# A broadcast maximum by way of DRAM instead of a matrix product, in a linear-attention and gated-FFN kernel

## The chip, the cores and the metric

The kernel runs on one core of one Trainium2 chip. The metric is the device time of one execution in microseconds, median of several runs. The kernel before takes 1002.14 us (three runs, 1001.49 to 1002.65).

The engines, by their names in the profile: PE is TensorE (matrix products; PEld is its weight load), DVE is VectorE, ACT is ScalarE, POOL is GpSimd, and SP is the sync engine, which here issues every DMA, in the order in which they are written. PSUM is the memory that PE writes products to, in eight banks; SBUF is the memory of the other operands.

## The reference

Linear attention with two softmaxes, then a gated feed-forward block, all in fp32:

```python
# q, k, v: (8 batches, 8 heads, 576 rows, 64)
q_s = exp(q - max(q, -1));  q_s /= sum(q_s, -1) + 1e-9
k_s = exp(k - max(k, 2));   k_s /= sum(k_s, 2) + 1e-9      # over the 576 rows, for each column
attn = einsum('bhsd,bhde->bhse', q_s, einsum('bhsd,bhse->bhde', k_s, v))
x = attn.transpose(0, 2, 1, 3).reshape(4608, 512)
xn = x / sqrt(mean(x*x, -1) + 1e-6) * rms_g
g = xn @ w_gate                                            # 512 x 1536
out = (g * sigmoid(g) * (xn @ w_val)) @ w_out              # 1536 x 512
```

The weights lie in DRAM as 64-bit words, which the kernel converts by itself.

## The kernel before

The 4608 rows are worked in nine blocks j of 512 rows, and the 1536 hidden columns in twelve slices of 128. A step s = 12 j + slice of the feed-forward part consists of f1.s.0 and f1.s.1 (gate and value, L839), twelve products each, and f2.s (the second product, L878). To get fp32 precision from the faster format (fp32r), every operand is split in a high part and a remainder: w_hi and w_lo for a slice of gate and value weights, o_hi and o_lo for the output weights, h_hi and h_lo for the hidden values, q_hi and q_lo for the queries, x_hi and x_lo for the block's input. A product is then three passes (high x high, high x low, low x high). The high parts are copies (L328), by default on ACT; the remainders are differences of two SBUF tensors (L816, L824, L860), by default or by the order on POOL. f2 is split when h_hi and h_lo of its step are in the order; for steps 0 to 3 they are not, and f2 multiplies the fp32 operands natively.

Between f1 and f2 stand g_mul (L844: gate from PSUM times the row factor, on DVE), silu (L848, ACT) and h_mul (L851: value from PSUM times that, DVE). f1 has two PSUM banks (ps_gv), one for gate and one for value, so that f1.s+1.0 waits for g_mul.s and f1.s+1.1 for h_mul.s.

Attention goes by batch b and pair of heads g (four pairs, 28 pairs in batches 1 to 7). For each, k_load fetches k into 116 partitions of five rows each, k_max (L461) takes the maximum of each partition's rows, k_tr (L486) transposes the 128 columns of the two heads to partitions, and k_top (L491) gives kx, one maximum for each of 128 columns, one to a partition. Every partition then needs all 128 of them in a row. Before, k_diag (L495, recorded as L333, on ACT) multiplies an identity matrix by kx, and k_rows (L500) multiplies a matrix of ones by that diagonal on PE, in native fp32; the result is read from PSUM by k_sub (L506, DVE), which subtracts it from k. k_exp (L510) takes the exponential, k_mm (L518) multiplies by v with a column of ones for the sum, and k_eps, k_rec and kv_hi, kv_lo (in batches 0 and 1: kv_norm0) normalise the result. q goes a similar way: q_max, q_half, q_max2, q_sub, q_exp, q_sum, q_half2, q_sum2, q_rec, q_mul, q_t, and q_x multiplies it with the normalised k-v product. x_sq, x_acc, n_sum and the steps n_t to n_cols give the row factors; store scales the block and writes it out.

In batches 2 to 7 the products of k are bundled in k_seg(m), one bank of PSUM each: k_mm of pair m - 2, k_rows of pair m - 1, k_tr of pair m. In batch 1 they are separate steps.

The order of the whole work is written out by hand, as a list of step names in a string (ORDER, some 2,800 names). Each engine executes its own steps in the order of the list; steps on different engines wait for each other's data and buffers alone. A suffix names the engine: `:A` ACT, `:D` DVE, `:P` POOL. conv_mul, conv_shift, conv_sign, conv_low and conv_add convert the weights during block 0; load_w loads them; warm is a product without use that fills PE's time.

Of the kernel before, what the change touches and what calls it, by code (L numbers as in the profile page):

```python
# [22 lines left out]
constants exp_table k_load.0.0 q_load0.0.0 v_ones.0.0 warm.9 k_load.0.2 kv_zero0.0 v_load.0.0 v_ones.0.2 v_ones.0.3  # L23
v_ones.0.1 kv_zero0.1 k_load.0.3 kv_zero.4 q_load0.0.3 kv_zero.5 kv_zero.6 kv_zero.7 k_load.0.1 kv_zero.0 q_load0.0.1
kv_zero.1 kv_zero.2 k_max0.0.0 v_load.0.2 kv_zero.3 q_max0.0.0 q_load0.0.2 k_tr.0.0 warm.2.0 k_top.0.0 q_sub0.0.0:P
v_load.0.3 k_diag.0.0:A k_rows.0.0 k_sub.0.0 warm.2.1 g_load q_exp.0.0 v_load.0.1 q_sum0.0.0 k_exp.0.0 load_w.0.0
k_max0.0.2 k_mm.0.0 load_w.0.1 load_w.1.0 q_eps0.0.0 k_max0.0.3 load_w.1.1 k_tr.0.2 warm.2.2 k_load.1.0 q_rec0.0.0
# [15 lines left out]
f1.0.1.1.2 f1.0.1.1.3 q_sum0.1.0 f1.0.0.2.0 f1.0.0.2.1 f1.0.0.2.2 w_hi.1.0.2:A n_y1.0 f1.0.0.2.3 f1.0.1.2.0 f1.0.1.2.1
f1.0.1.2.2 conv_low.1.2.1 w_lo.1.0:P f1.0.1.2.3 conv_low.3.0.2 conv_sign.0.2 w_lo.1.1:P n_rows.0 k_tr.1.0
conv_low.3.2.1 k_top.1.0 g_mul.0 conv_add.0.2.1 k_diag.1.0:A k_rows.1.0 n_cols.0 f1.1.0 silu.0 q_eps0.1.0 load_w.4.0
k_sub.1.0 load_w.4.1 v_ones.1.1 q_rec0.1.0 load_w.4.2 k_max.1.1 q_mul0.1.0:P conv_mul.2.0 v_load.1.1 conv_mul.2.1
h_mul.0 k_exp.1.0 conv_shift.2.0 f1.1.1 conv_shift.2.1 q_load0.1.3 conv_sign.2.0 conv_low.2.2.1 conv_sign.2.1
# [10 lines left out]
conv_sign.5.0 w_lo.4.1:P x_sq.1.0 x_lo.1.0 conv_mul.5.1 f1.4.0 conv_add.5.2.1 q_sum0.1.2 o_hi.4:A h_mul.3 conv_mul.6.0
o_lo.4:P conv_shift.5.1 conv_low.6.0.2 conv_shift.6.0 o_hi.5:A q_eps0.1.1 f1.4.1 conv_sign.5.1 conv_low.7.2.1 o_lo.5:P
q_rec0.1.1 g_mul.4 conv_mul.6.1 conv_sign.6.0 silu.4 q_mul0.1.1:P conv_shift.6.1 k_tr.1.1 conv_add.5.0.2 f2.3  # L60
q_load.2.0 k_top.1.1 conv_sign.6.1 k_diag.1.1:A conv_low.6.2.1 h_mul.4 conv_mul.6.2 h_hi.4:A conv_add.6.0.2
conv_shift.6.2 w_hi.5.0.2:A conv_sign.6.2 k_rows.1.1 warm.2.13 conv_low.8.0.2 load_w.10.0 k_sub.1.1 q_t0.1.1
load_w.10.1 k_max.1.3 load_w.10.2 w_lo.5.0:P f1.5.0 k_exp.1.1 q_c0.1.1:D w_lo.5.1:P q_max.2.0 w_hi.6.0.2:A q_half.2.0
h_lo.4:P k_mm.1.1 conv_mul.7.0 g_mul.5 f2.4 k_load.2.1 w_lo.6.0:P q_exp.1.3 k_eps.1.1 conv_shift.7.0 silu.5 k_rec.1.1
conv_sign.7.0 conv_add.6.2.1 kv_norm0.1.1:D q_sum0.1.3 conv_mul.7.1 f1.6.0 w_lo.6.1:P conv_mul.7.2 conv_shift.7.1
o_hi.6:A v_ones.1.3 q_eps0.1.2 conv_sign.7.1 v_load.1.3 conv_low.10.0.2 o_lo.6:P q_rec0.1.2 conv_shift.7.2 q_x0.1.1
conv_low.8.2.1 g_mul.6 q_mul0.1.2:P conv_low.10.2.1 conv_sign.7.2 f1.5.1 conv_add.7.0.2 x_hi.1.1:A q_load.2.1 x_sq.1.1
# [872 lines left out]
```

## Time and profile before

| | |
|---|---|
| median of three runs | 1002.14 us |
| the profiled execution | 1001.34 us, of which the span from first to last instruction is 999.5 us |
| PE busy | 982.6 us, 4897 instructions |
| POOL, ACT, DVE busy | 738.0, 612.5, 468.8 us |
| granted clock of PE | 0.999 of full speed |
| DMA | 57.64 MB, 58 GB/s on average; 233 to 285 GB/s in each of the first three of 40 slices |

The views give, for a group of equal instructions: line, engine, operation, output <- inputs with their shapes, the count, then busy us and mean ns of one, then the idle time of the engine ahead of them and what ended it. A timeline gives the start in us, the length in us, and the instruction. Matmuls are pipelined: the length of one reaches into the next, so that the cost of one is read from start to start.

### The profile page before, as it was taken

The numbers are of one execution on the slowest core, as the hardware profiler recorded it, in microseconds if no ns is written. First come the engines' busy times: TensorE is split into PE (matmuls) and PEld (weight loads), VectorE is DVE, ScalarE is ACT, GpSimd is POOL, SyncE is SP. The second block draws the span as 40 slices with busy tenths as digits, with TensorE's granted clock in tenths as the row PEclk, the third lists the DMA queues.
The fourth block names the chain that finished last, engine by engine and source line by source line (L and its number), as shares of the span: only waits on it lengthen the run. The fifth ranks groups of instructions, "written<-read, shape, count | busy, mean of one in ns | idle before, by whom it ended". The sixth has DMA issues, their size and how long they took to land.

```text
span 999.5 us, 14416 instructions
## 1 busy us (share of the span) xinstructions
PE 982.6 (98%) x4897; PEld 797.1 (80%) x4897; DVE 468.8 (47%) x1135; ACT 612.5 (61%) x885; POOL 738.0 (74%) x643
## 2 busy tenths in 40 slices
PE   7899999999999999999999999999999999999998
PEld 5567887888888888888888888888888888888886
...
GB/s 237 233 285 187 148 36 78 52 39 35 35 76 36 35 13 83 41 35 11 77 36 35 35 56 56 36 35 23 75 5 9 1 43 1 1 0 43 1 1 43
DMA packets 129687, 57.64 MB, mean 58 GB/s; under 512 B 101797, under 2 KB 123597, under 8 KB 129613
## 3 DMA queue, kind: packets, MB, share of 16 engines
...
## 4 chain that ended last, share of the span: by engine, by line
PE 92%; DMA 3%; SPq 2%; DVE 2%; issue 0%; ACT 0%; POOL 0%; ACTq 0%; POOLq 0%; DVEq 0%
PE ps_gv L839 57%; PE ps_o L878 29%; PE ps_a L717 2%; PE ps_a L518 2%; DMA raw<-in_moe_w_out_dram 2%; DMA kt<-in_k_dram 1%; PE ps_a L500 1%; SPq L364 1%; DMA qt<-in_q_dram 0%; PE ps_a L646 0%; SPq L600 0%; PE ps_a L767 0%; SPq L450 0%; PE ps_a L486 0%; DVE cm L461 0%
## 5 line engine op out<-in xcount | busy, mean ns | idle before, releaser
L816 POOL TENSOR_TENSOR wl<-w,wh 128x512 fp32r<-128x512 f32 x216 | 278.7, 1297 | 103.9 <-ACT wh L328 102.3
L839 PE MATMUL ps_gv<-xh,wh 128*128 128x512 f32 x864 | 236.5, 395 | 2.9 <-ACT kt L510 1.7
L839 PE MATMUL ps_gv<-xl,wh 128*128 128x512 f32 x864 | 231.3, 390 | 0.0
L839 PE MATMUL ps_gv<-xh,wl 128*128 128x512 f32 x864 | 231.1, 389 | 0.0
L839 PEld LDWEIGHTS ps_gv<-xl,wh 128*128 128x128 f32 x864 | 162.2, 188 | 34.7 <-issue 0.2
L839 PEld LDWEIGHTS ps_gv<-xh,wl 128*128 128x128 f32 x864 | 162.1, 188 | 34.2
L839 PEld LDWEIGHTS ps_gv<-xh,wh 128*128 128x128 f32 x864 | 159.7, 188 | 37.1 <-ACT kt L510 2.1
L848 ACT ACTIVATE gs<-gs 128x512 f32<-128x512 f32 x108 | 68.3, 632 | 164.5 <-DVE gs L844 164.0
L844 DVE TENSOR_TENSOR gs<-ps_gv,r 128x512 f32<-128x512 f32 x108 | 74.1, 686 | 192.1 <-PE ps_gv L839 168.8
L824 POOL TENSOR_TENSOR ol<-w,oh 128x512 fp32r<-128x512 f32 x104 | 135.1, 1299 | 37.7 <-ACT oh L328 37.7
L860 POOL TENSOR_TENSOR hl<-gs,hh 128x512 fp32r<-128x512 f32 x104 | 134.7, 1296 | 29.5 <-ACT hh L328 29.5
L851 DVE TENSOR_TENSOR gs<-ps_gv,gs 128x512 f32<-128x512 f32 x108 | 74.5, 690 | 144.1 <-PE ps_gv L839 123.8
L328 ACT CAST wh<-w 128x1024 fp32r<-128x1024 f32 x108 | 113.1, 1047 | 29.2 <-PE ps_gv L839 28.2
L328 ACT CAST oh<-w 128x512 fp32r<-128x512 f32 x104 | 64.3, 618 | 83.3 <-PE ps_o L878 83.3
L878 PE MATMUL ps_o<-oh,hh 128*128 128x512 f32 x416 | 114.0, 394 | 0.0
L878 PE MATMUL ps_o<-oh,hl 128*128 128x512 f32 x416 | 112.0, 390 | 0.0
L878 PE MATMUL ps_o<-ol,hh 128*128 128x512 f32 x416 | 111.9, 389 | 0.0
L878 PEld LDWEIGHTS ps_o<-oh,hl 128*128 128x128 f32 x416 | 78.1, 188 | 16.7 <-POOL hl L860 0.2
L878 PEld LDWEIGHTS ps_o<-ol,hh 128*128 128x128 f32 x416 | 78.1, 188 | 16.6
L328 ACT CAST hh<-gs 128x512 fp32r<-128x512 f32 x104 | 64.4, 619 | 43.2 <-DVE gs L851 42.0
L878 PEld LDWEIGHTS ps_o<-oh,hh 128*128 128x128 f32 x416 | 76.8, 188 | 15.3 <-issue 0.4
L848 ACT ACT_TABLE_LOAD x43 | 55.2, 1283 | 0.8
...
## 6 DMA issues: line engine op xcount, KB each, us to landing
...
```

The source lines that it names most:

```text
L328: (e.copy if e is nc.scalar else e.tensor_copy)(dst, src)
L364: nc.sync.dma_start(t.rearrange("p (c f) -> p c f", c=NKT), src)
L518: nc.tensor.matmul(ps[h * D:(h + 1) * D, :D + 1], lhsT=ke[:n, h, j], rhs=vt[:n, j, h], start=(j == 0), stop=(j == len(rows) - 1))
L717: nc.tensor.matmul(px[:, c0:c1], lhsT=wt, rhs=mv[:, c0:c1], start=(i == 0), stop=(i == 2))
L816: on(nc.gpsimd).tensor_tensor(out=wl[:, a], in0=W(s % NF, a), in1=wh[:, a].bitcast(F32), op=ALU.subtract)
L824: on(nc.vector).tensor_tensor(out=ol, in0=W(s % NF, 2), in1=wo_[s][0].bitcast(F32), op=ALU.subtract)
L839: nc.tensor.matmul(pd[s], lhsT=m[:, a, c * P:(c + 1) * P], rhs=X[j, c][x], start=(n == 1), stop=(n == 3 * NKT))
L844: nc.vector.tensor_tensor(out=gs, in0=g_[s], in1=r_[s // NF], op=ALU.mult)
L848: nc.scalar.activation(g_[s], g_[s], AF.Silu)
L851: nc.vector.tensor_tensor(out=g_[s], in0=v_[s], in1=g_[s], op=ALU.mult)
L860: on(nc.gpsimd).tensor_tensor(out=hl, in0=g_[s], in1=h_[s][0].bitcast(F32), op=ALU.subtract)
L878: nc.tensor.matmul(po[t], lhsT=a[:, t * P:(t + 1) * P], rhs=w, start=(i == 0 and n == 0), stop=(i == NF - 1 and n == len(terms) - 1))
```

## The change

- The maxima of batches 1 to 7 reach all partitions by DMA. k_put writes kx (128 words, one in each partition) to a line in DRAM, and k_get reads that line back into all 116 partitions at once. Both are issued by SP. k_diag and k_rows remain for batch 0 alone (4 of 32 pairs). k_seg keeps k_mm and k_tr.
- k_sub reads the maxima from SBUF, so that it can be on any engine: 20 of the 28 go to POOL, 8 stay on DVE. The tile of the maxima takes a buffer of `cm`, which has three in place of two.
- f2 of steps 2 and 3 becomes split (h_hi, h_lo, o_hi, o_lo of both steps are added); f2 of steps 0 and 1 stays native: two native second products in place of four.
- The order is another one up to about step 33 and nearly the old one behind that. In it 57 steps have gone from POOL to DVE and 29 from ACT to DVE (w_lo 19, o_lo 9, h_lo, q_mul 7 each, x_acc, q_lo 5 each, q_sub 3, q_sub0, n_lo; w_hi 8, h_hi 6, o_hi 5, kv_hi 5, x_hi 3, q_hi, one store), and q_c0.1.1, x_hi.1.0 and kv_norm0.1.1 from DVE to ACT.

```diff
+    dram = ctx.enter_context(tc.tile_pool(name="dram", bufs=4, space=bass.MemoryType.DRAM))
...
     def k_max(b, g):
-        cm = ap.tile([P, P], F32, name="cm")[:KP if b else P0].rearrange("p (h d) -> p h d", h=2)
+        cm = ap.tile([P, P], F32, name="cm", bufs=3)[:KP if b else P0].rearrange("p (h d) -> p h d", h=2)
...
         if m >= 2:
             k_mm(*at(m - 2), t)
-        if 0 < m <= NG * (B - 2):
-            k_rows(*at(m - 1), t)
         if m < NG * (B - 2):
-            k_tr(*at(m), t[:, 2 * P:])
+            k_tr(*at(m), t[:, P:])
...
+    def k_put(b, g):
+        row_[b, g] = dram.tile([P, 1], F32, name="row")
+        nc.sync.dma_start(row_[b, g], kx_[b, g])
+
+    def k_get(b, g):
+        mb = ap.tile([P, P], F32, name="cm", bufs=3)[:KP]
+        nc.sync.dma_start(mb, row_[b, g].rearrange("p o -> o p").broadcast_to([KP, P]))
+        mb_[b, g] = mb.rearrange("p (h d) -> p h d", h=2)
```

The order around one segment of the steady part (the steps of k from one k_seg to the next, with the products of PE between them; other steps left out):

```diff
-k_seg.12 f1.42.0 k_eps.4.2 k_load.5.1 k_top.5.0 k_rec.4.2 k_diag.5.0:A k_sub.4.3 kv_hi.4.2:A k_exp.4.3 kv_lo.4.2
-q_x.4.2 v_load.5.0 f1.42.1 k_max.5.1 q_load.5.3 f2.41 f1.43.0 f1.43.1 f2.42 f1.44.0 f1.44.1 k_seg.13
+k_seg.12 f1.42.0 k_load.5.1 k_eps.4.2 k_top.5.0 k_rec.4.2 kv_hi.4.2:A k_put.5.0 kv_lo.4.2 q_x.4.2 v_load.5.0
+f1.42.1 k_max.5.1 k_get.5.0 f2.41 q_load.5.3 f1.43.0 f1.43.1 k_sub.5.0:P k_exp.5.0 f2.42 f1.44.0 f1.44.1 k_seg.13
```

And around the first three pairs of batch 1, again with the steps of k and PE alone:

```diff
-k_tr.1.0 k_top.1.0 k_diag.1.0:A k_rows.1.0 f1.1.0 k_sub.1.0 k_exp.1.0 f1.1.1 f2.0 f1.2.0 f1.2.1 f2.1 k_mm.1.0 f1.3.0
-k_tr.1.1 f2.3 k_top.1.1 k_diag.1.1:A k_rows.1.1 k_sub.1.1 f1.5.0 k_exp.1.1 k_mm.1.1
-k_tr.1.2 f1.6.1 k_top.1.2 k_diag.1.2:A k_rows.1.2 f1.7.0 k_sub.1.2 k_exp.1.2 f2.5 f1.7.1 k_mm.1.2
+k_tr.1.0 k_top.1.0 f1.1.0 load_w.4.2 k_put.1.0 load_w.2.2 f1.1.1 f2.0 load_w.4.1 k_get.1.0 f1.2.0 k_sub.1.0:D
+f2.1 f1.2.1 f1.3.0 k_exp.1.0 f1.3.1 f2.2 f1.4.0 k_mm.1.0 f1.4.1
+k_tr.1.1 k_top.1.1 f1.5.1 f1.6.0 f1.6.1 k_put.1.1 k_get.1.1 k_sub.1.1:D f1.7.0 k_exp.1.1 k_mm.1.1
+k_tr.1.2 k_top.1.2 k_put.1.2 k_get.1.2 f1.8.1 f2.7 k_sub.1.2:D f1.9.0 k_exp.1.2 k_mm.1.2
```

More of the change, by code (lines that the diff above doesn't have):

```diff
@@ L22 @@
 ORDER = """
[L23 to L27, printed above, removed]
@@ L43 @@
[L43 to L47, printed above, removed]
@@ L58 @@
[L58 to L67, printed above, removed]
@@ L273 @@
[L273 to L276 removed]
+constants v_ones.0.2 kv_zero.3 kv_zero0.0 k_load.0.0 kv_zero.1 v_ones.0.0 exp_table warm.9 k_max0.0.0 k_tr.0.0
@@ new lines @@
+silu.39 f1.39.1 k_eps.4.1 k_load.5.0 v_ones.4.3 k_top.4.3 k_rec.4.1 q_sum2.5.1 q_rec.5.1 q_mul.5.1:P k_put.4.3
+kv_hi.4.1:A v_load.4.3 kv_lo.4.1 f2.38 w_hi.41.0.2:A h_mul.39 k_max.5.0 h_hi.39:A w_lo.41.0:P k_get.4.3 h_lo.39:P
+q_x.4.1 o_hi.40:A f1.40.0 w_lo.41.1:P x_hi.4.1:A q_t.4.3 x_sq.4.1 x_lo.4.1 q_load.5.2 q_hi.4.3:A o_lo.40:P x_acc.4.1:P
+f1.40.1 g_mul.40 silu.40 k_sub.4.3:P q_lo.4.3:P k_exp.4.3 f2.39 h_mul.40 q_max.5.2 h_hi.40:A q_half.5.2 w_hi.42.0.2:A
+h_lo.40:P f1.41.0 o_hi.41:A w_lo.42.0:P w_lo.42.1:P f1.41.1 g_mul.41 o_lo.41:P silu.41 q_max2.5.2 q_sub.5.2:P f2.40
@@ new lines @@
+h_mul.41 w_hi.43.0.2:A h_hi.41:A w_lo.43.0:P q_exp.5.2 h_lo.41:P k_seg.12 o_hi.42:A q_sum.5.2 f1.42.0 w_lo.43.1:P
+k_load.5.1 k_eps.4.2 k_top.5.0 k_rec.4.2 q_half2.5.2 o_lo.42:P kv_hi.4.2:A k_put.5.0 kv_lo.4.2 v_ones.5.0 q_sum2.5.2
+q_x.4.2 v_load.5.0 q_rec.5.2 g_mul.42 q_mul.5.2:P f1.42.1 k_max.5.1 x_hi.4.2:A x_sq.4.2 silu.42 x_lo.4.2 x_acc.4.2:P
+k_get.5.0 q_t.5.0 f2.41 q_load.5.3 w_hi.44.0.2:A h_mul.42 h_hi.42:A w_lo.44.0:P h_lo.42:P f1.43.0 o_hi.43:A
+w_lo.44.1:P o_lo.43:P f1.43.1 g_mul.43 q_max.5.3 silu.43 k_sub.5.0:P q_half.5.3 q_max2.5.3 k_exp.5.0 q_sub.5.3:P f2.42
@@ new lines @@
+f2.47 k_eps.5.0 k_load.5.3 v_ones.5.2 h_hi.48:A w_lo.50.0:P k_top.5.2 k_rec.5.0 kv_hi.5.0:A h_lo.48:P kv_lo.5.0
+k_put.5.2 v_load.5.2 q_x.5.0 w_lo.50.1:P store.3.0:A store.3.1:A f1.49.0 k_max.5.3 x_hi.5.0:A x_sq.5.0 x_lo.5.0
+o_hi.49:A q_t.5.2 o_lo.49:P f1.49.1 q_hi.5.2:A g_mul.49 k_get.5.2 q_lo.5.2:P q_load.6.1 silu.49 store.3.2:A f1.50.0
+h_mul.49 w_hi.51.0.2:A k_sub.5.2:P store.3.3:A h_hi.49:A w_lo.51.0:P k_exp.5.2 f2.48 g_mul.50 h_lo.49:P q_max.6.1
+silu.50 w_lo.51.1:P q_half.6.1 f1.50.1 q_max2.6.1 o_hi.50:A q_sub.6.1:P o_lo.50:P q_exp.6.1 f2.49 h_mul.50 h_hi.50:A
@@ new lines @@
+q_sum.6.1 w_hi.52.0.2:A h_lo.50:P q_half2.6.1 f1.51.0 w_lo.52.0:P o_hi.51:A w_lo.52.1:P o_lo.51:P k_seg.15 g_mul.51
+silu.51 f1.51.1 k_eps.5.1 k_load.6.0 v_ones.5.3 k_top.5.3 k_rec.5.1 q_sum2.6.1 q_rec.6.1 q_mul.6.1:P k_put.5.3
+kv_hi.5.1:A v_load.5.3 kv_lo.5.1 f2.50 w_hi.53.0.2:A h_mul.51 k_max.6.0 h_hi.51:A w_lo.53.0:P k_get.5.3 h_lo.51:P
+q_x.5.1 o_hi.52:A f1.52.0 w_lo.53.1:P x_hi.5.1:A q_t.5.3 x_sq.5.1 x_lo.5.1 q_load.6.2 q_hi.5.3:A o_lo.52:P x_acc.5.1:P
+f1.52.1 g_mul.52 silu.52 k_sub.5.3:P q_lo.5.3:P k_exp.5.3 f2.51 h_mul.52 q_max.6.2 h_hi.52:A q_half.6.2 w_hi.54.0.2:A
@@ new lines @@
+h_lo.52:P f1.53.0 o_hi.53:A w_lo.54.0:P w_lo.54.1:P f1.53.1 g_mul.53 o_lo.53:P silu.53 q_max2.6.2 q_sub.6.2:P f2.52
+h_mul.53 w_hi.55.0.2:A h_hi.53:A w_lo.55.0:P q_exp.6.2 h_lo.53:P k_seg.16 o_hi.54:A q_sum.6.2 f1.54.0 w_lo.55.1:P
+k_load.6.1 k_eps.5.2 k_top.6.0 k_rec.5.2 q_half2.6.2 o_lo.54:P kv_hi.5.2:A k_put.6.0 kv_lo.5.2 v_ones.6.0 q_sum2.6.2
+q_x.5.2 v_load.6.0 q_rec.6.2 g_mul.54 q_mul.6.2:P f1.54.1 k_max.6.1 x_hi.5.2:A x_sq.5.2 silu.54 x_lo.5.2 x_acc.5.2:P
+k_get.6.0 q_t.6.0 f2.53 q_load.6.3 w_hi.56.0.2:A h_mul.54 h_hi.54:A w_lo.56.0:P h_lo.54:P f1.55.0 o_hi.55:A
```

477 lines of the change are left out of this document (237 added, 240 removed).

## The prediction

> **What bounds the kernel now.** I read the page first: busy time by engine, then the chain that ended last.
>
> ```profile
> span 999.5 us, 14416 instructions
> PE 982.6 (98%) x4897; PEld 797.1 (80%) x4897; DVE 468.8 (47%) x1135; ACT 612.5 (61%) x885; POOL 738.0 (74%) x643
> PE 92%; DMA 3%; SPq 2%; DVE 2%; issue 0%; ACT 0%; POOL 0%; ACTq 0%; POOLq 0%; DVEq 0%
> ```
>
> TensorE is busy for 982.6 of 999.5 us, and 92% of the chain is its own work. A stage view says where the missing 16.9 us lie.
>
> ```profile
> 0.00:41.00 41.00, 32.35 (x203) 20.79 (x203) 31.01 (x81) 29.79 (x52) 24.87 (x48) 1.00 1.02 263
> 41.00:154.00 113.00, 110.29 (x529) 83.01 (x528) 83.47 (x158) 92.00 (x134) 103.23 (x82) 1.00 0.53 153
> 166.00:341.00 175.00, 175.00 (x912) 144.76 (x911) 94.74 (x255) 118.38 (x168) 138.22 (x121) 1.00 0.21 48
> 341.00:990.00 649.00, 649.00 (x3173) 536.27 (x3172) 248.30 (x612) 360.53 (x514) 460.30 (x383) 1.00 0.12 30
> 990.00:999.50 9.50, 5.63 (x25) 4.22 (x23) 1.93 (x3) 2.47 (x4) 1.29 (x1) 0.94 0.31 110
> ```
>
> After the window come busy us of PE, PEld, DVE, ACT and POOL. From 166 to 990 us PE has no hole: there only work taken off PE shortens the span, and a step moved between other engines is worth nothing while they keep up. The holes lie at the start (8.65 us to 41, 2.7 to 154) and at the end (3.9, the last store), which the change leaves. In the start other engines are nearly as full: POOL 103 of 113 us, ACT 92, DVE 83. The waits of PE after its first 40 us are four:
>
> ```profile
> PE ps_gv L839 <- ACT kt L510: 1.7, 1, 1.7
> PE ps_a L500 <- ACT cm L333: 1.7, 1, 1.7
> PE ps_a L518 <- DVE w L385: 1.3, 1, 1.3
> PE ps_gv L839 <- DVE gs L851: 1.2, 1, 1.2
> ```
>
> **Part 1: the product k_rows goes from PE.** In the steady part k_rows (L500) stands in k_seg between k_mm (L518) and k_tr (L486); the timeline of PE there, start and length:
>
> ```profile
> 288.25 0.80 PE L518 MATMUL ps_a<-vt,kt 116*64 116x65 f32 x20
> 288.98 0.48 PE L500 MATMUL ps_a<-cm,ones 128*116 128x128 f32 x2
> 289.29 0.26 PE L486 MATMUL ps_a<-ident,cm 116*128 116x116 f32 x1
> 289.32 1.17 PE L839 MATMUL ps_gv<-xh,wh 128*128 128x512 f32 x4
> ```
>
> Matmuls overlap, so the price is from start to start: k_rows holds PE for 289.29 - 288.98 = 0.31 us; the transpose behind it only 0.03. With k_rows out, the transpose follows k_mm. The trace has 28 such products of two instructions each; those of batch 1 stand between f1 matmuls:
>
> ```profile
> L500 PE MATMUL ps_a<-cm,ones 128*116 128x128 f32 x56 | 12.9, 313 | 1.7 <-ACT cm L333 1.7
> 40.72 0.48 PE L500 MATMUL ps_a<-cm,ones 128*116 128x128 f32 x2 [1.67 <-ACT cm L333]
> 40.95 1.18 PE L839 MATMUL ps_gv<-xh,wh 128*128 128x512 f32 x4
> 129.68 0.38 PE L500 MATMUL ps_a<-cm,ones 128*116 128x128 f32 x2
> 129.82 0.70 PE L839 MATMUL ps_gv<-xh,wh 128*128 128x512 f32 x2
> ```
>
> That is 0.23 us for the first and 0.14 for the later ones. Of the 24 in k_seg I take 22 at 0.31 and the two at the ends, where no k_mm or no k_tr stands beside them, at 0.23: 7.3 us. Batch 1: 0.23 + 3 x 0.14 = 0.65. Together **7.9 us** of PE. The first also takes its wait for k_diag with it, **1.7 us**: nothing on PE waits for the line now but k_mm, which has been moved from ahead of f1.3.0 to behind f1.4.0.
>
> **Part 2: two second products change their form.** f2 of steps 2 and 3 was native fp32 (8 instructions); with h_hi, h_lo, o_hi and o_lo added it becomes 12 of the split kind. Steps 0 and 1 stay native. The chain has both forms; the first two rows are steps 2 and 3:
>
> ```profile
> 66.10 3.45 PE ps_o L878 x8
> 79.43 3.44 PE ps_o L878 x8
> 118.80 2.72 PE ps_o L878 x12
> ```
>
> 2 x (3.445 - 2.72) = **1.5 us** less on PE. It costs the other engines eight steps of the start, priced below.
>
> **Part 3: the line through DRAM.** k_put writes 128 words, k_get reads them into 116 partitions, both on SP's queue. The trace has no such pair; nearest rows:
>
> ```profile
> 719.87 0.61 SPq L452 DMA_DIRECT2D vt<-in_v_dram  x1
> 996.75 0.33 SPq L893 DMA_DIRECT2D out_dram<-gs  x1
> 1.67 4.24 DMA qt<-in_q_dram
> SPq L425 <- PE ps_a L518: 323.5, 24, 25.6
> ```
>
> Issue of a small DMA: 0.33 to 0.61 us. The last write to DRAM is issued by 997.1 and the span ends at 999.5, so a write lands within 2.4 us; a read at the crowded start took 4.24. So put and get need at most 0.6 + 2.4 + 0.6 + 4.2 = 7.8 us, at least the two issues, 0.7; I take 6, nearer the upper end, since both landings are of DMAs far larger than a line but of the same kind. On SP, k_get waits for the put to land and holds what is queued behind it: from batch 5 on that is a q_load, which nothing needs at once (k_put waits for k_top, with v_load behind it; the cm buffer that k_get takes was freed a segment before), and SP has spare time (323.5 us of waiting for buffers that k_mm frees). From k_put.5.0 to k_sub.5.0 the order has f1.42.1, f2.41, f1.43.0, f1.43.1: 4 x 2.72 = 10.9 us, and the five issues of v_load between run while the put lands. Counted so, the cover in batches 4 to 7 is 9 us or more but for 4.1 (5.4 us) and 5.1, 6.1, 7.1, 7.3 (6.3, two f1 and a q_x). At 6 us only 4.1 falls short, by 0.6; at 7.8 POOL would stand in k_sub, with w_lo and h_lo behind it, for 2.4 + 4 x 1.5 = 8.4 us in all. I price it at **zero** on PE: POOL is idle for 29% of that stretch (460 of 649 us busy), which takes up such a stand. A gain is excluded, PE having no hole. In batches 1 to 3 some distances are shorter (rival 2).
>
> **Part 4: steps moved between engines.** k_sub reads its maximum from SBUF now; 20 of 28 go to POOL. 57 steps of POOL (19 w_lo, 10 or fewer each of o_lo, h_lo, q_mul, x_acc, q_lo and others) and 29 of ACT (8 w_hi, 6 h_hi, 5 o_hi and others) go to VectorE, all before f1.33.
>
> ```profile
> L816 POOL TENSOR_TENSOR wl<-w,wh 128x512 fp32r<-128x512 f32 x216 | 278.7, 1297 | 103.9 <-ACT wh L328 102.3 <-PE ps_a L767 1.6
> L844 DVE TENSOR_TENSOR gs<-ps_gv,r 128x512 f32<-128x512 f32 x108 | 74.1, 686 | 192.1 <-PE ps_gv L839 168.8 <-POOL ol L824 12.4 <-POOL wl L816 10.3
> L506 DVE TENSOR_TENSOR kt<-kt,ps_a 116x640 f32<-116x640 f32 x28 | 22.5, 805 | 0.8 <-PE ps_a L500 0.8
> L669 POOL TENSOR_TENSOR qt<-qt,st 128x512 f32<-128x512 f32 x28 | 29.4, 1053 | 18.5 <-DVE st L666 15.6 <-issue 2.2 <-POOL ol L824 0.3
> L333 ACT ACTIVATE cm<-ident,kx 128x128 f32<-128x128 f32 x32 | 12.8, 400 | 17.0 <-DVE kx L491 12.8 <-DVE rs L540 3.9
> ```
>
> A difference of 128x512 is 1.30 us on POOL and, by the g_mul row, about 0.69 on DVE; a k_sub is 0.81 on DVE and, scaling the 1.05 us of q_sub by 640/512, 1.3 on POOL; ACT loses 28 k_diag of 0.40, which no wait of PE but the first hung on. After 341 us that is +1.3 us on POOL in each 24 us, where POOL is 71% busy: nothing. In 41 to 154 us (up to f1.13) 15 POOL and 6 ACT steps come to DVE, and o_lo.3: about 16 x 0.69 + 3 x 1.0 (w_hi, twice as wide) + 3 x 0.6 = 16 us, less some 3 for three steps that DVE gives to ACT and one k_sub: 83.5 + 13 = 96.5 us. POOL is relieved: 103.2 - 15 x 1.3 + about 5 = 89. But such an operation on DVE, with both tensors in SBUF, is not always that short:
>
> ```profile
> 573.98 1.30 POOL L824 TENSOR_TENSOR ol<-w,oh 128x512 fp32r<-128x512 f32 x1
> 574.28 1.03 DVE L684 SCALAR_TENSOR_TENSOR sm<-sm,sw 128x16 f32<-128x16 f32 x1
> L684 DVE SCALAR_TENSOR_TENSOR sm<-sm,sw x28: 130/166/1026, 153.7 to 762.1; 128x16 f32<-128x16 f32 x28
> L844 DVE TENSOR_TENSOR gs<-ps_gv,r x108: 625/691/693, 40.0 to 987.5; 128x512 f32<-128x512 f32 x108
> ```
>
> An addition of 16 columns takes 0.17 us at the median, and 1.03 when POOL is in the middle of an operation: it ends as POOL's does (575.31 and 575.28). L844, which has one input in PSUM, never passes 0.69. So each of the 20 two-SBUF operations that DVE has up to f1.13 (k_sub of 1.0, 1.1, 1.2 and 2.0 among them) may wait on average half of 1.3 us, times POOL's load there of 0.8 to 0.9: 0.55 us, 11 us in all. 96.5 + 11 = 107.5 us for DVE in a stage in which PE will have 113.0 - 2.7 - 1.5 - 0.4 = 108 us of work. That is no room, and g_mul and h_mul, which free PE's banks, queue on DVE behind whatever waits. In 166 to 341 the same count gives 94.7 + 44 + 46 x 0.52 = 163 of 175 us: some room. Bounds of what this costs PE: nothing if the waits fall into DVE's holes (and the 4.2 us of other PE waits may go too, so -4), 11 us if all of the first stage's reach PE. I take **+2.5**, nearer the lower end, since f1 and f2 between a bank's last write and its next use give g_mul 2.7 to 5.4 us of slack and one wait is at most 1.3.
>
> The Trainium skill (SBUF — State Buffer, "Who interferes with whom") states it as a rule: a VectorE instruction with two SBUF inputs contends with a GpSimd instruction that reads SBUF, and the later one stands still until the first is through. The rows above agree. Taken for every one of the 66 such operations it gives rival 1.
>
> **The sum.** The profiled execution took 1001.34 us (span 999.5 and 1.84 around it): 1001.34 - 7.9 - 1.7 - 1.5 + 2.5 = 992.7. The median of the runs is 1002.14, 0.8 above it, so the forecast is **993.5 us**.
>
> **The rivals.** (1) *DVE becomes the bound of the first third.* 66 two-SBUF operations x 0.65 us x 0.8 = 34 us of standing still. For it: the loads just counted. Against: 46 of them lie where DVE has room. If a quarter of it, 8.6 us, reaches PE: 1002.1 - 11.1 + 8.6 = 999.6.
> (2) *Slower: the line comes late.* For six k_sub of the start the order leaves little PE work between put and use: 1.1 none, 1.2 and 1.3 5.4 us, 2.0 3.7, 2.1 2.7, 3.1 1.0. (Only the sequence on each engine binds, so the put may go earlier than this count has it.) At 6 us a line DVE or POOL would stand 6 + 0.6 + 0.6 + 2.3 + 3.3 + 5 = 17.8 us, with g_mul, h_mul or w_lo behind, and load_w unissued behind k_get on SP. It decides from where 11.1 of the 17.8, five eighths, reach PE; at four fifths, 14.2: 1002.1 - 11.1 + 14.2 = 1005.2. Against: k_top.1.1 stands three products ahead of its put, so SP may be free for it early, and the DMA engines are half idle (share 0.53 from 41 to 154 us).
> (3) *The start loses its holes too.* POOL, 91% busy to 154 us, is relieved, and the three remaining waits (4.2 us) go, with no new ones: 1002.1 - 11.1 - 4.2 + 0.6 = 987.4.
> (4) *It does nothing*: PE bound by something that k_rows only covered. The start-to-start times speak against it.
>
> **How the numbers follow.** A difference under 0.2% (2 us) cannot be told from none here. Forecast, 991 to 997: 0.58. Rival 3, below 991: 0.17. Rival 1, 997 to 1000: 0.10. Between 1000.1 and 1004.1, rivals 1 and 2 in part, or 4: 0.07. Rival 2, above that: 0.08. Faster 0.85, same 0.07, slower 0.08. The range 987 to 1000 leaves out the lower third of rival 3 and what lies above, 0.2.
>
> **What would show it.** L500 left with batch 0 only; start to start 0.73 us from k_mm to the transpose; two rows of f2 with x8 instead of four; PE busy some 9 us less. PE waits after 41 us of 5 us in sum bear out +2.5; waits of L839 for gs (g_mul, h_mul) with L816, L824 or L860 on DVE longer than 1 us are rival 1; waits of DVE or POOL in L506 for the DMA of cm are rival 2. A hole in PE after 341 us would make part 3 wrong.

## The result and the profile after

The change is slower: a median of 1056.88 us (1054.42 to 1060.41, four runs) beside 1002.39 us (1001.49 to 1002.94, four runs) for the kernel before on the same chip, a ratio of 1.0549 [1.0531, 1.0568]. The forecast was 993.5. The profiled execution of after took 1054.42 us. The page first (span, busy time by engine, chain), the lines that answer to the first ones of the prediction:

```profile
span 1052.4 us, 14340 instructions
PE 995.2 (95%) x4849; PEld 803.7 (76%) x4849; DVE 533.8 (51%) x1202; ACT 576.9 (55%) x830; POOL 712.7 (68%) x609
PE 65%; DMA 16%; DVE 7%; SPq 5%; issue 2%; ACT 2%; POOL 2%; DVEq 0%; ACTq 0%; POOLq 0%
```

PE has 48 products fewer (4849 for 4897) and yet is busy 12.6 us longer. DMA has gone from 3% of the chain to 16%. The holes of PE, span less busy time, have grown from 16.9 to 57.2 us. The stages of the prediction (window; busy us of PE, PEld, DVE, ACT, POOL; granted clock; DMA share; GB/s):

```profile
0.00:41.00 41.00, 33.48 (x197) 22.06 (x198) 31.14 (x82) 28.21 (x49) 23.04 (x43) 1.00 1.02 258
41.00:154.00 113.00, 95.19 (x434) 73.68 (x433) 79.31 (x139) 73.49 (x110) 78.45 (x61) 0.91 0.59 144
166.00:341.00 175.00, 159.57 (x782) 128.23 (x779) 129.16 (x297) 81.79 (x117) 89.67 (x76) 0.94 0.26 49
341.00:990.00 649.00, 641.32 (x3149) 526.19 (x3148) 277.44 (x663) 368.05 (x520) 487.31 (x406) 1.00 0.14 34
```

Two things are new. PE has holes of 17.8 us from 41 to 154, of 15.4 from 166 to 341 and of 7.7 behind that, where it had 2.7 and none. And the granted clock is 0.91 and 0.94 in the first two of these stages, where it was 1.00 in both. Around two of the holes, windows of 10 us show the two together:

```profile
100.00:110.00 10.00, 3.31 (x25) 2.84 (x26) 5.57 (x12) 4.22 (x5) 1.54 (x2) 0.63 0.77 225
250.00:260.00 10.00, 5.89 (x17) 4.32 (x16) 7.71 (x20) 5.36 (x8) 3.21 (x3) 0.66 0.20 39
```

The hole of the first is shown further below (8.61 us); that of the second is this one in PE's timeline:

```profile
253.98 0.55 PE L728 MATMUL ps_a<-qh,kv_hi 128*128 128x256 f32 x1 [3.34 <-DVE kv_lo L571]
```

The chain that ended last has the put itself in it, with its length (start, length):

```profile
41.12 9.05 DMA row<-kx
89.22 7.43 DMA row<-kx
123.42 7.07 DMA row<-kx
238.45 7.67 DMA row<-kx
352.18 9.31 DMA row<-kx
```

A put takes 7 to 9 us, here counted from its issue to the issue of the read that waits for it. (The first row is the put of pair 1.0, the second that of 1.1.) The timelines of SP and then POOL show one line in the steady part, pair 4.1, for which the prediction had counted 5.4 us of cover, the least of all in batches 4 to 7, and 6 us of need:

```profile
395.24 0.44 SPq L497 DMA_DIRECT2D row<-kx  x1
395.78 2.88 SPq L454 DMA_DIRECT2D vt<-in_v_dram  x4
398.70 0.61 SPq L456 DMA_DIRECT2D vt<-in_v_dram  x1
403.54 0.27 SPq L501 DMA_DIRECT2D cm<-row  x1
407.69 1.57 POOL L517 TENSOR_TENSOR kt<-kt,cm 116x640 f32<-116x640 f32 x1 [3.48 <-DMA cm<-row]
```

From put to read 8.3 us, of which SP stands still for 4.2 (399.31 to 403.54); from read to k_sub 4.2 us; 12.5 in all, and POOL stands for 3.48. Pair 5.0, for which the prediction had counted 10.9 us of cover, has its put at 469.51, its read at 477.52 and its k_sub, 11.7 us behind the put, here:

```profile
481.21 1.57 POOL L517 TENSOR_TENSOR kt<-kt,cm 116x640 f32<-116x640 f32 x1 [0.48 <-DMA cm<-row]
```

With that cover POOL stands for 0.48 only. In the start the line takes longer, with less cover and more behind it. These are SP's, DVE's and PE's rows for pair 1.1:

```profile
96.72 0.29 SPq L501 DMA_DIRECT2D cm<-row  x1
104.33 0.82 DVE L517 TENSOR_TENSOR kt<-kt,cm 116x640 f32<-116x640 f32 x1 [10.19 <-DMA cm<-row]
106.69 1.44 PE L529 MATMUL ps_a<-vt,kt 116*64 116x65 f32 x20 [8.61 <-ACT kt L521]
```

The put of 89.22 releases the read at 96.72; k_sub starts 7.6 us later, DVE having stood for 10.19 us, and k_mm, behind k_exp, leaves PE a hole of 8.61. The waits by group say whom the line and the transfers beside it held up in all (us in total, times, longest):

```profile
POOL kt L517 <- DMA cm<-row: 72.3, 16, 6.3
DVE st L663 <- DMA qt<-in_q_dram: 65.0, 18, 5.7
DVE kt L517 <- DMA cm<-row: 31.0, 5, 10.2
ACT ot L337 <- DMA out_dram<-ot: 18.3, 4, 5.0
PE ps_a L529 <- ACT kt L521: 16.4, 2, 8.6
PE ps_o L889 <- ACT ot L337: 7.4, 8, 1.2
SPq L501 <- DMA row<-kx: 110.2, 24, 7.6
```

The second and the fourth row are not about the line at all: q and the stores land late. The row for PE L889 is a hole at the end of a block of rows, behind 341 us, since ACT cannot reuse `ot` until a store has gone out. These 7.4 us are nearly all of PE's holes of 7.7 there: behind 341 us the standing of POOL in k_sub costs PE nothing.

### The profile page after: what moved, and what is told of

It is laid out like the page before. It is cut to its first block, busy times and chain, and to the rows that moved or that the text cites. A ratio compares the mean times of both kernels' runs of the same rounds, so it can differ in the third digit from the quotient of the medians.

```text
span 1052.4 us, 14340 instructions
## 1 busy us (share of the span) xinstructions
PE 995.2 (95%) x4849; PEld 803.7 (76%) x4849; DVE 533.8 (51%) x1202; ACT 576.9 (55%) x830; POOL 712.7 (68%) x609
## 2 busy tenths in 40 slices
DMA packets 137076, 59.29 MB, mean 56 GB/s; under 512 B 105940, under 2 KB 130988, under 8 KB 137004
## 3 DMA queue, kind: packets, MB, share of 16 engines
q1 hardware_dynamic: 137004, 58.39, 23.6%
## 4 chain that ended last, share of the span: by engine, by line
PE 65%; DMA 16%; DVE 7%; SPq 5%; issue 2%; ACT 2%; POOL 2%; DVEq 0%; ACTq 0%; POOLq 0%
PE ps_gv L850 40%; PE ps_o L889 21%; DMA row<-kx 5%; DMA kt<-in_k_dram 3%; DMA out_dram<-ot 3%; SPq L597 2%; DMA cm<-row 2%; PE ps_a L728 2%; PE ps_a L529 2%; SPq L454 1%; DMA qt<-in_q_dram 1%; DMA raw<-in_moe_w_val_dram 1%; DMA w<-in_k_dram 1%; DMA raw<-in_moe_w_gate_dram 1%; DMA raw<-in_moe_w_out_dram 1%
## 5 line engine op out<-in xcount | busy, mean ns | idle before, releaser
L827 POOL TENSOR_TENSOR wl<-w,wh 128x512 fp32r<-128x512 f32 x197 | 258.0, 1315 | 92.4 <-ACT wh L332 82.9
L850 PE MATMUL ps_gv<-xh,wh 128*128 128x512 f32 x864 | 240.9, 400 | 5.8 <-DVE xh L339 3.4
L850 PE MATMUL ps_gv<-xl,wh 128*128 128x512 f32 x864 | 235.1, 393 | 0.0
L871 POOL TENSOR_TENSOR hl<-gs,hh 128x512 fp32r<-128x512 f32 x99 | 129.7, 1310 | 37.9 <-ACT hh L332 26.9
L835 POOL TENSOR_TENSOR ol<-w,oh 128x512 fp32r<-128x512 f32 x96 | 126.3, 1316 | 15.3 <-ACT oh L332 10.7
L889 PE MATMUL ps_o<-oh,hh 128*128 128x512 f32 x424 | 119.7, 400 | 7.4 <-ACT ot L337 7.4
L332 ACT CAST wh<-w 128x1024 fp32r<-128x1024 f32 x100 | 104.5, 1045 | 25.3 <-PE ps_gv L850 21.9
L889 PE MATMUL ps_o<-ol,hh 128*128 128x512 f32 x424 | 115.0, 392 | 0.0
L889 PE MATMUL ps_o<-oh,hl 128*128 128x512 f32 x424 | 114.6, 391 | 0.0
L889 PEld LDWEIGHTS ps_o<-oh,hh 128*128 128x128 f32 x424 | 80.0, 192 | 26.0 <-ACT ot L337 10.3
L517 POOL TENSOR_TENSOR kt<-kt,cm 116x640 f32<-116x640 f32 x20 | 31.2, 1560 | 93.0 <-DMA cm<-row 72.3
L889 PEld LDWEIGHTS ps_o<-ol,hh 128*128 128x128 f32 x424 | 80.2, 189 | 17.1
L889 PEld LDWEIGHTS ps_o<-oh,hl 128*128 128x128 f32 x424 | 80.2, 189 | 17.1 <-POOL hl L871 0.2
```

The source lines that it names most:

```text
L332: (e.copy if e is nc.scalar else e.tensor_copy)(dst, src)
L517: on(nc.vector).tensor_tensor(out=ke, in0=ke, in1=mb_[b, g].unsqueeze(2).broadcast_to([n, 2, c, D]), op=ALU.subtract)
L827: on(nc.gpsimd).tensor_tensor(out=wl[:, a], in0=W(s % NF, a), in1=wh[:, a].bitcast(F32), op=ALU.subtract)
L835: on(nc.vector).tensor_tensor(out=ol, in0=W(s % NF, 2), in1=wo_[s][0].bitcast(F32), op=ALU.subtract)
L850: nc.tensor.matmul(pd[s], lhsT=m[:, a, c * P:(c + 1) * P], rhs=X[j, c][x], start=(n == 1), stop=(n == 3 * NKT))
L871: on(nc.gpsimd).tensor_tensor(out=hl, in0=g_[s], in1=h_[s][0].bitcast(F32), op=ALU.subtract)
```

## The experiments

All are told by their median in us, with the ratio to the kernel before on the same chip (1001.4 to 1002.3 us).

**x1, the line alone, in the order of before.**

```diff
 (order of before, batches 2 to 7)
-k_diag.b.g  ... k_rows in k_seg
+k_put.b.g   ... v_load.b.g k_get.b.g
```

> The order of before, with one part of the change alone: the pairs of batches 2 to 7 take the line through DRAM. k_put stands where k_diag stood, k_get right behind the v_load of the same pair, and k_sub stays where it was, on DVE, one whole segment (24 us) later; batch 1 and all four native f2 stay. Theory L (the line takes some 12 us from put to use, and the new order left less): a segment covers it, so only the gain on PE is left: 22 x 0.31 + 2 x 0.23 = 7.3 us less, 995.1 (994 to 997), no hole in PE behind 166 us. Rival R (the differences moved to DVE stand against POOL): there are none here but 24 k_sub of 0.8 us, so also about 995. Rival S (SP standing in k_get for the put, and so every load behind it, is what costs): SP stands some 4 us in each of 24 segments here too, q is late, PE shows holes at q_x: 1003 or more.

Measured 1036.46, 1.0333 [1.0316, 1.0351]. That the line is only late is refuted: here k_sub follows a whole segment later, it waits for the line 7.6 us in all (2 times), and the kernel still loses 34 us. The loss sits in what SP could not issue or the queue could not deliver: DVE waits 107.4 us for q (37.9 before).

**x2, after, without the wait for the put** (the read takes words that lie in DRAM from the start; the puts stay).

```diff
-        nc.sync.dma_start(mb, row_[b, g].rearrange("p o -> o p").broadcast_to([KP, P]))
+        nc.sync.dma_start(mb, rms_g.rearrange("(o p) -> o p", p=P)[0:1].broadcast_to([KP, P]))
```

> The kernel after, with k_get reading 128 words of rms_g in place of the line, so that it waits for no put; the maxima that k_sub subtracts are therefore other numbers. All else is as after, the puts too. Theory L: of the 12 to 15 us between put and k_sub the 7 to 9 of the put go, and with them most of the standing of DVE and POOL in k_sub, SP's standing, the holes of PE behind it and the slow clock: 1000 (994 to 1006). Rival R: the moved differences are all still there: 1045 or more. Rival S: as L, since SP does not stand either; x1 tells those two apart.

**x3, as x2, with the read issued right behind k_load** into a tile of its own, so that nothing waits for the line.

```diff
-k_put.b.g v_load.b.g ... k_get.b.g
+k_load.b.g k_get.b.g ... k_put.b.g v_load.b.g
```

> As x2 (k_get reads words of rms_g, so k_sub subtracts other numbers), and k_get is issued right behind the k_load of its pair, into tiles of its own, so that nothing waits for the put or for the get; the puts stay. What is left of the change is its order, its moves between engines and what PE saves. Theory L: the terms of the forecast without the line: 993 (989 to 997). Rival R: 1040 or more. If it comes out between 997 and 1010, the order and the moves cost something of their own besides the line.

Measured 1040.64, 1.0383 [1.0333, 1.0433], and 1036.35, 1.0336 [1.0313, 1.0358]. Both miss what theory L gave (994 to 1006 and 989 to 997). Taking every wait on the line away gives back 20 of 54 us. The puts, which nobody reads in x3, are still there.

**x4, after, with 90 moved steps back on their old engines.**

```diff
-w_lo.7.1:D  o_lo.7:D  q_mul.2.0:D  w_hi.11.0.2:D
...
+w_lo.7.1:P  o_lo.7:P  q_mul.2.0:P  w_hi.11.0.2:A
...
```

> The kernel after, with every step that the new order had moved to another engine back on its old one (57 to POOL, 29 to ACT, three to DVE, and o_lo.3 on POOL); k_sub stays as after. The line and the order are those of after. Theory L: the standing in k_sub stays, and POOL, which runs 20 of them, is fuller: 1050 to 1065. Rival R: the contention is gone: 1010 or less.

Measured 1069.90, 1.0678 [1.0636, 1.0720], 13 us more than after (theory L had 1050 to 1065): the moves are not the fault, they help.

**y1, x3 without the puts.** The order, the moves and the 28 reads of the change stay. (This expectation and that of z5 say 127 rows; the read has 116.)

```diff
-k_put.b.g   (all 28)
```

> The kernel of x3_line_early with its 28 puts taken out: the order and the moves of the change, the 28 spread reads (127 x 512 bytes, of words that lie in DRAM from the start), no wait for a put. The output is not the reference's: k_sub subtracts other numbers than the maxima, as in x3. Theory D (each put, 128 writes of 4 bytes, holds what is queued behind it on SP's DMA queue for about 5 us, so that v, q and the stores land late): 993 to 1003 us, close to what was forecast for the change, and the waits of PE for ot (11.6 us in x3) back to before's. Rival O (the order and the moves themselves, or the reads, cost): about 1030 us, as x3, with the same waits.

Measured 994.09, 0.9926 [0.9909, 0.9944]. Removing 28 transfers of 512 bytes, which no step reads, gives back 42 us. DVE's wait for q falls to 10.4 us (55.4 in x3, 65.0 in after), and ACT's for a store to 0.2 (27.1 and 18.3). The first lines of y1's page:

```profile
span 992.5 us, 14296 instructions
PE 976.8 (98%) x4849; PEld 793.9 (80%) x4849; DVE 530.5 (53%) x1202; ACT 582.9 (59%) x830; POOL 717.2 (72%) x609
```

The same 4849 products keep PE busy for 976.8 us here and for 995.2 in after. So the 59.9 us between the two spans are 18.4 of longer products and 41.5 of holes. Most of the 18.4 is the slower clock, which came with the holes (its mean is 1.000 here and 0.979 in after): in after the granted clock is 0.50 in six stretches of 3.4 to 10.2 us, in which PE is busy for 30.1 us, and at full clock that work would take 15.1 us less. The other 3.3 us are not explained. The windows of x3 and of y1 differ in the share of the DMA engines, too (100 to 154 us; the second to last column is the DMA share):

```profile
100.00:154.00 54.00, 45.71 (x223) 34.73 (x222) 41.76 (x72) 33.28 (x51) 34.89 (x26) 0.97 0.62 100
```

```profile
100.00:154.00 54.00, 51.99 (x261) 40.62 (x261) 49.94 (x92) 40.18 (x62) 39.26 (x28) 1.00 0.35 85
```

With three puts among them the packets took 62% of the engines' time for 100 GB/s; without, 35% for 85. This holds for x3 alone: in after, which has two puts in this window, the share is 0.37. What the puts do in each kernel is to hold up the transfers behind them. SP's own waits in x3 name the puts although no step reads them; by these rows, issuing a load or a q behind a put had to wait until it was through:

```profile
SPq L597 <- DMA row<-kx: 34.7, 13, 4.8
SPq L454 <- DMA row<-kx: 11.2, 3, 4.4
```

**y2, before with 24 puts that nobody reads.**

```diff
 k_diag.b.g:A
+k_put.b.g    (b = 2 to 7; nothing else changed)
```

> The kernel before, word for word, with 24 puts that nobody reads, each right behind k_diag of batches 2 to 7; the products k_rows stay and the output is the reference's. Theory D: the puts alone make it 1015 to 1030 us (24 puts that each delay the transfers behind them by 5 us, of which some 1 us each reaches PE, plus the slow clock after the holes). Rival W (it is the waiting for the put and the late read that cost, not the put): 1002 to 1006 us. Rival O gives 1002 as well, since the order is before's.

Measured 1012.34, 1.0105 [1.0090, 1.0120]: slower by 10.5 us, less than the theory said, but nothing except the puts can be the reason. DVE's waits for q go from 37.9 to 101.1 us, most of it hidden in this order (first before, then y2):

```profile
DVE st L652 <- DMA qt<-in_q_dram: 37.9, 16, 3.8
DVE st L658 <- DMA qt<-in_q_dram: 101.1, 22, 10.0
```

**y3, x1 with the put issued by ACT.**

```diff
-        nc.sync.dma_start(row_[b, g], kx_[b, g])
+        nc.scalar.dma_start(row_[b, g], kx_[b, g])
```

> x1_old_order_line (before's order, the line in batches 2 to 7; 1036.5 us) with the put issued by ACT instead of SP; the reads stay on SP and wait as before. If the put holds up the queue that it is in (D), SP's transfers no longer stand behind it, but SP still stands until the put has landed: 1010 to 1025 us. If 128 small writes clog the DMA engines for every queue: 1030 to 1040, and the time from put to read stays at 7 to 9 us. If only SP's standing counts (W): about 1036, too.

Measured 1034.62, 1.0329 [1.0277, 1.0382], as x1: another queue is no help, and SP still waits 93.6 us for puts (103.1 in x1). By the time alone that could still be SP's standing. The packets of a v_load (288 KB, issued by SP) decide it: in z1, told below, where no put of single words is ahead of it; in after, behind the put that SP issued at 395.24; and in y3, behind the put that ACT issued at 422.14:

```profile
386.00:388.00 2.00, 2.00 (x11) 1.64 (x10) 1.81 (x3) 1.31 (x3) 1.49 (x2) 1.00 0.65 149
```

```profile
397.00:405.00 8.00, 8.00 (x37) 6.60 (x36) 4.85 (x10) 5.04 (x7) 7.10 (x6) 1.00 0.14 32
```

```profile
424.00:432.00 8.00, 8.00 (x40) 6.72 (x39) 3.71 (x8) 3.74 (x6) 6.36 (x6) 1.00 0.15 32
```

The load runs at 149 GB/s for 2 us in z1 and at 32 GB/s for 8 us in the other two, with a DMA share of 0.14 and 0.15: behind such a put the packets come slowly while the engines are mostly not busy, and in y3 the load is not in the put's queue. So what a put holds up is not only the queue that it was put in. The Trainium skill says as much (DMA: Bandwidth & Descriptors, "Issuing engines are not separate DMA queues"): transfers started by different engines run on the same 16 DMA engines. This run agrees with it.

**y4, x1 with the put as four rows.** DVE turns the column into four rows of 32 words first.

```diff
+        sq = small.tile([P, 32], F32, name="sq")
+        nc.vector.transpose(sq, kx_[b, g])
-        row_[b, g] = dram.tile([P, 1], F32, name="row")
-        nc.sync.dma_start(row_[b, g], kx_[b, g])
+        row_[b, g] = dram.tile([4, 32], F32, name="row")
+        nc.sync.dma_start(row_[b, g], sq[0:P:32])
```

> x1_old_order_line with the 128 maxima laid out as 4 rows of 32 first (one transpose of 32x32 blocks on DVE, some 0.1 us) and put as 4 writes of 128 bytes instead of 128 writes of 4; the read and the order are those of x1. Output as the reference's. Theory D: the put lands in 2 to 3 us instead of 7 to 9 and holds up nothing: 1002 to 1010 us. Rival W (any line through DRAM makes SP stand and its loads late): put to read still 4 us or more, 1020 to 1036 us.

Measured 996.35, 0.9950 [0.9934, 0.9967]: 40 us less than x1, less than the 1002 to 1010 that theory D gave, and 5.5 us less than before. SP's waits for the put, in x1 and then in y4:

```profile
SPq L499 <- DMA row<-kx: 103.1, 23, 9.4
```

```profile
SPq L510 <- DMA row<-sq: 5.0, 5, 1.0
```

**z2, z6 and u1: what of the put is slow.** All three are x3 with another put that nobody reads: 128 rows of 512 bytes of a constant tile (z2), the same 128 words 512 bytes apart (z6), and 64 bytes apart (u1).

```diff
-        row_[b, g] = dram.tile([P, 1], F32, name="row")
-        nc.sync.dma_start(row_[b, g], kx_[b, g])
+        row_[b, g] = dram.tile([P, P], F32, name="row")
+        nc.sync.dma_start(row_[b, g], ident)               # z2
+        nc.sync.dma_start(row_[b, g][:, 0:1], kx_[b, g])   # z6; u1 with a tile of [P, 16]
```

> x3_line_early with each put made 128 rows of 512 bytes (64 KB of a constant tile, so that it does not wait for k_top either) instead of 128 words of 4 bytes: the same number of packets, 128 times the bytes. The output is not the reference's, as in x3. If small writes are what costs (T or E): 994 to 1003 us. If any write of 128 rows to DRAM at this place in the queue costs: 1025 to 1040 us, as x3.

> x3_line_early (1036.4 us; the puts are in the queue and nobody reads them) with the 128 words of a put written 512 bytes apart instead of side by side. The output is not the reference's, as in x3. Theory T (the writes of 4 bytes are slow because many of them fall into the same short stretch of DRAM and wait for each other): 994 to 1005 us. Rival E (every write of 4 bytes to DRAM is slow by itself, or 128 packets are): 1025 to 1040 us.

> z6_put_spaced (994.6 us; the 128 words of a put 512 bytes apart, nobody reads them) with the words 64 bytes apart, 8 to a stretch of 512. The output is not the reference's, as in x3. If the writes collide only within 64 bytes: 994 to 996 us. If they collide within 512 bytes: the put lies between the two, some 1000 to 1020 us.

Measured 994.86 (0.9926 [0.9898, 0.9955]), 994.62 (0.9921 [0.9892, 0.9950]) and 993.92 (0.9921 [0.9903, 0.9939]): all as y1, which has no put. So neither 128 packets nor writes of 4 bytes cost anything here; 128 writes of 4 bytes side by side cost 42 us. All that is left of SP's waits for puts in z6, and z6's stage in which x3 had a clock of 0.98 and a DMA share of 0.73:

```profile
SPq L611 <- DMA row<-kx: 0.8, 1, 0.8
```

```profile
41.00:154.00 113.00, 110.20 (x538) 85.07 (x537) 102.24 (x175) 88.80 (x132) 92.95 (x72) 1.00 0.58 160
```

The Trainium skill (DMA: Bandwidth & Descriptors, "Specifications") has a transfer under 512 bytes done as read and write back. As the whole explanation that falls: the 4-byte writes of u1 and z6 are as small as those of x3, and as many (137,004 packets on SP's queue in all three). The writes collide when they lie less than 64 bytes apart; distances between 4 and 64 bytes were not tried. Whether they wait for each other in the DMA engines or in the memory no run shows; a put into SBUF was not tried.

**z1 and z5, after with the put of y4**, and in z5 the read over 128 partitions besides.

```diff
-        mb = ap.tile([P, P], F32, name="cm", bufs=3)[:KP]
+        mb = ap.tile([P, P], F32, name="cm", bufs=3)    # z5; read into all 128, k_sub uses 116
```

> The changed kernel with the put of y4 (the 128 maxima turned into 4 rows of 32 on DVE, written as 4 writes of 128 bytes); all else, the order and the moves too, as in the change. Theory P (the put of 128 writes of 4 bytes is what was wrong, in its own time and in what it holds up): put to read 1.6 us as in y4, the whole line about 6 us as the prediction had it, 993 to 1000 us. Rival W (k_sub still waits too long for the read, 4 to 5 us, above all in the start): 1003 to 1015 us.

> z1_after_row_put with the read spread over all 128 partitions instead of 127 (one row more, that nobody uses). If the read of 127 rows is slow because of its odd number of partitions (it cannot be dealt out evenly to 16 DMA engines), read to k_sub falls from 4 to 5 us to about 2, and the time by 1 to 4 us below z1; if it is slow because all rows are read from the same 512 bytes, or if it is hidden anyway, as z1.

Measured 1009.32 (1.0077 [1.0052, 1.0103]) and 1008.59 (1.0057 [1.0039, 1.0074]). The fast put takes 47.6 us off the change; 7 us more than before remain, as rival W had it (theory P had 993 to 1000), and the number of rows read is not the reason. In z1 the windows show PE busy throughout from 300 to 1000 us; what is left of the loss lies ahead of that. Timeline rows of SP, DVE and PE for pair 1.1 of z1:

```profile
93.34 0.55 SPq L508 DMA_DIRECT2D row<-sq  x1
95.00 0.30 SPq L512 DMA_DIRECT2D cm<-row  x1
101.06 0.83 DVE L528 TENSOR_TENSOR kt<-kt,cm 116x640 f32<-116x640 f32 x1 [7.75 <-DMA cm<-row]
103.43 1.44 PE L540 MATMUL ps_a<-vt,kt 116*64 116x65 f32 x20 [6.29 <-ACT kt L532]
```

From put to read it is 1.7 us now, where after had 7.5; but the read itself, among the loads of weights, still takes 6.1 us, and PE has 6.29 us of its 8.61 still to wait.

**v1, z1 with batch 1's line made free**, and **z4, x3 with the puts of batch 1 alone.**

```diff
 v1: -k_put.1.g k_get.1.g   +k_load.1.g k_get.1.g (words of rms_g)
 z4: -k_put.b.g for b = 2 to 7
```

> z1_after_row_put (1009.3 us) with the line of batch 1 made free: its 4 puts are left out and its reads take words of rms_g right behind k_load, so that k_sub waits for nothing; batches 2 to 7 go as in z1. The output is not the reference's in batch 1, where other numbers than the maxima are subtracted. If what is left of the loss is the wait for the line in the start: 994 to 998 us. If the read costs in every batch: 1003 to 1009 us.

> x3_line_early (1036.4 us) with the puts of batches 2 to 7 taken out: only the 4 puts of batch 1, in the stage from 60 to 150 us where the weights are loaded, stay. The output is not the reference's, as in x3. If the puts of the start cost most (their window has a DMA share of 0.62 against 0.35 without puts): 1010 to 1020 us. If each of the 28 costs about the same: 994 + 4 x 1.5 = 1000 us.

Measured 1001.68 (0.9999 [0.9986, 1.0012]) and 1001.87 (1.0004 [0.9988, 1.0021]). v1 falls between the two expectations: of the 15.2 us from y1 to z1, half comes with the line of batch 1 and half with the lines of the batches behind. In z4 four puts cost 7.8 us, 1.9 each, so that the other 24 cost 34.5 or 1.4 each: the start is worse, but not the whole of it.

**v3, y1 with the 90 moves undone.** The edit is that of x4.

> y1_gets_only (994.1 us; no line to wait for) with the 90 steps that the change moved to another engine back on the engines they had before. The output is not the reference's, as in y1. The prediction's term (the moves cost 2.5 us, for DVE beside POOL is slower): 990 to 992.5 us. Rival (POOL is the engine that is late, and the moves relieve it): 996 to 1004 us, with POOL's wl and hl later and PE waiting for them.

Measured 1000.93, 0.9992 [0.9981, 1.0003]: the moves save 6.8 us where no line disturbs.

**v2 and w1: is there more in it?** y4 with the second products of steps 2 and 3 split, and y4 with 89 of the moves.

```diff
 v2: +h_hi.2:A h_lo.2:P o_hi.2:A o_lo.2:P  +h_hi.3:A h_lo.3:P o_hi.3:A o_lo.3:D
 w1: -w_lo.7.1:P o_lo.7:P q_mul.2.0:P ...  +w_lo.7.1:D o_lo.7:D q_mul.2.0:D ...
```

> y4_row_put (996.4 us; before's order, the line with the fast put in batches 2 to 7) with the second products of steps 2 and 3 split as in the change (o_hi, o_lo, h_hi, h_lo of these steps added, o_lo of step 3 on DVE, o_hi and o_lo of step 5 behind the product of step 3). Output as the reference's. By the prediction's term of 1.5 us: 994 to 995.5 us. Rival (ACT, POOL and DVE are full in this stage, and the eight added instructions make PE wait): 997 to 1003 us.

> y4_row_put (996.4 us; before's order, the line with the fast put in batches 2 to 7, all products as before) with the 89 steps that the change moved to another engine moved here too, k_sub left on DVE. Output as the reference's. If the moves help by themselves, because POOL was late: 990 to 994.5 us. If they belong to the order that was made for them: 996 to 1005 us.

Measured 1008.33 (1.0073 [1.0060, 1.0087]) and 1013.52 (1.0118 [1.0098, 1.0139]), 12 and 17 us more than y4, and beyond both expectations of each. The moves help in the order that was made for them and hurt in the other; the split steps, put into before's order by hand, cost more than they save. y4 is the version to keep: 996.35.

## Why the prediction was wrong

The medians give the balance. Order, moves, split products and the work taken off PE, with a line that costs nothing: 1002.4 to 994.1 (y1), -8.3. The wait for a line that is put fast: +15.2 (z1). The put as 128 adjacent words: +47.6 (after).

- **Part 3 is the step that failed.** "At least the two issues, 0.7; I take 6" for a line, and "I price it at zero on PE". Measured 12.5 and 11.7 us in the steady part (pairs 4.1 and 5.0) and 15.1 in the start (pair 1.1, 89.22 to 104.33), beyond the upper bound of 7.8. The bound was built from landings of transfers "far larger than a line but of the same kind"; they are not of the same kind, since none of them writes 128 single words side by side. For the waiting alone the zero held in the steady part: behind 341 us of after PE does not wait for k_sub, and with the fast put, in z1, it is busy throughout from 300 to 1000 us. What the term left out is that a put costs those who do not read it: in x3 nobody reads, and the puts cost 42 us through the transfers behind and beside them. The hole in PE after 341 us that the prediction named as the sign against part 3 is there, 7.7 us, and it is PE waiting for late stores. The prediction looked at what k_get holds up on SP's queue, not at what the put does to the DMA engines.
- **Rival 2 named the place in the start, and too small a price.** It had 6 us a line and a break-even at 11.1 us. k_sub did wait for the DMA of cm, 31.0 us on DVE and 72.3 on POOL, and pair 1.1, for which the rival had counted no cover at all, made a hole of 8.61. By z1 the line, even with a fast put, costs 15 us, near the 14.2 that the rival took, but half of that is in batch 1 (v1), and a line there takes 7.7 us (93.34 to 101.06 in z1), not 6. The rival did not have the puts' effect on q and the stores.
- **The clock was left out.** The Trainium skill (TensorE: Matmul & The Clock Gate, "Part 1") has the clock fall back to half after some 3.4 us without work. The size agrees, a clock of 0.50; the time is shorter here: in the hole of 3.34 us that ends at 253.98 the clock is 1.00 up to 252.88, which is 2.2 us into the hole, and 0.50 from there to 259.70. Of the 59.9 us between the spans of after and y1, some 15 are this slower clock. A price for holes in the start has to carry this: here about 0.4 us for each us of hole (15.1 for 41.5).
- **Part 1 was right in kind, a little large in size.** The first product behind the segment comes 0.82 us after k_mm, as in the rows of y1 below, for 1.07 in the kernel before: 0.25 to 0.26 us saved, not 0.31, since the transpose takes 0.09 us behind k_mm and not 0.03. For 24 segments that is 6.1 for 7.3 us. The 0.73 us from k_mm to the transpose that the prediction asked for is there.

```profile
368.37 0.80 PE L526 MATMUL ps_a<-vt,kt 116*64 116x65 f32 x20
369.10 0.32 PE L485 MATMUL ps_a<-ident,cm 116*128 116x116 f32 x1
369.19 1.17 PE L886 MATMUL ps_o<-oh,hh 128*128 128x512 f32 x4
```

- **Part 2 happened as foreseen** within the change: in the chain of y1 two rows of the second product have eight instructions and the third has twelve.

```profile
48.20 3.43 PE ps_o L886 x8
54.37 3.43 PE ps_o L886 x8
66.87 2.75 PE ps_o L886 x12
```

- **Part 4 had the wrong sign.** DVE does wait for POOL: a w_lo on DVE (L827, in the rows of after below) has a mean of 0.95 us, 0.90 in y1, where the prediction had 0.69 and a wait of 0.55. This fits the rule of the Trainium skill (SBUF — State Buffer, "Who interferes with whom"), with less than half of the wait. L695, the addition of 16 columns (L684 in before), has a mean of 723 ns in after and 333 in before, but the moves are not what lengthens it: it has 387 in y1 and 516 in v3, without the moves. Relieving POOL and ACT was worth more: v3 puts the moves at -6.8 us, not +2.5; how much of that is POOL and how much ACT was not tried apart. Rival 1 with its 999.6 us did not come about.
- **That y1 lies within a us of the forecast is partly luck.** v3 is the change without a line to wait for and without the moves: 1000.9, 0.8 below before, where parts 1 and 2 and PE's wait for k_diag promised 11.1. Of the 10.3 us that are missing, 3.6 are the size of parts 1 and 2 (PE's busy time fell by 5.8 us in y1, not by 9.4), and the 6 to 7 that remain fall, by subtraction alone, to the new order and the 28 reads, for which the sum had no term. The 9.3 us by which part 4 was off make up for them.

```profile
L695 DVE SCALAR_TENSOR_TENSOR sm<-sm,sw 128x16 f32<-128x16 f32 x28 | 20.2, 723 | 0.2
L827 DVE TENSOR_TENSOR wl<-w,wh 128x512 fp32r<-128x512 f32 x19 | 18.0, 947 | 2.8 <-ACT wh L332 2.6
L517 POOL TENSOR_TENSOR kt<-kt,cm 116x640 f32<-116x640 f32 x20 | 31.2, 1560 | 93.0 <-DMA cm<-row 72.3 <-DMA qt<-in_q_dram 9.2 <-DVE ps_a L800 6.8
```

What stays open: why a put costs 1.4 to 1.9 us in the change's order and 0.4 in that of before. In x3 PE waits for `ot` at the ends of the blocks and in y2 it does not, so that the order before has more slack for late stores; that is argued, not shown.
